# A last third of the tokens moved behind the attention: 72 interleaved items become 48 and three 512-token units, in a new written order

## The chip, the core and the metric

The kernel runs on one core of a Trainium2 chip. The metric is the device time of one execution in microseconds (us). Three runs of the kernel before gave 606.1, 606.41 and 606.9 us, median 606.41. Profiles are of one execution each, taken by the hardware profiler.

## The reference

An mLSTM attention (2 batches, 8 heads, 768 steps, head size 40) feeds two feed-forward layers, all in float32:

```python
for t in range(S):                       # attention, for each batch and head
    m_new = maximum(f[t] + m, i[t])
    C = exp(f[t] + m - m_new) * C + exp(i[t] - m_new) * outer(v[t], k[t])
    n = exp(f[t] + m - m_new) * n + exp(i[t] - m_new) * k[t]
    y[t] = sigmoid(o[t]) * (C @ q[t]) / maximum(abs(n @ q[t]), 1)
x = y as (1536, 320)
for e in range(4):                       # 320 -> 1024 -> 320, weighted by token
    out += p[:, e:e+1] * (maximum(x @ w1[e], 0) @ w2[e])
result = ((out @ w_a) * (out @ w_b)) @ w_out     # 320 -> 1536 -> 320
```

## The kernel before

**Tiles and chunks.** The 1536 tokens are 12 tiles of 128: tile n = 2j + b is chunk j (0 to 5) of batch b. The attention works chunk by chunk, since a chunk needs the state of the one before. The expert layer has 8 blocks of 512 hidden features, the last layer 6 blocks of 256. Every product is made of float32 values split into a rounded part (names in h: `xh`, `wh`, `hh`) and a rest (names in l), with three products for one.

**Two forms of the expert layer.** In the first stage blocks 0 to 2 are worked as *items* (class `Item`): one block, one group of 128 features, 256 tokens. An item has a first half (`a`, 8 matmuls of 256 columns, then `hh` on ScalarE and `hl` on VectorE) and a second half (`b`, 2 x 3 matmuls of 320 columns into `psy`). `Stream` lets the second halves run two items behind the first. The `psa` tiles of first halves have two PSUM banks, so the first half of item k needs the bank that `hl` of item k-2 has read. Twelve items cover 256 tokens, 72 all of them. In the second stage, from block 3 on, the work goes in *units* of one block and 512 tokens (`quad_a`, `quad_b`), in which two matmuls of 64 rows stand side by side.

**The order.** The attention steps lie between the items by a list `ev` of (time, step, arguments), line 711 on. A time k + 0.0 to k + 0.5 puts a step between the first half of item k and the second half of item k-2, a later one behind that second half. Each engine works what it gets strictly in this order, and so do the DMA queues of SP, ScalarE and GpSimd. For chunks 3 to 5 the list is made by a loop: chunk j is spread over twelve items that begin at 12 (j-1).

**Steps of one tile from chunk 2 on.** `load_qk` (DMA, three buffers), `split_qk` (ScalarE, line 356, rounds q and k into `qs`), four `low_qk` (VectorE or GpSimd, line 362, subtract the rounded values), `scores` (TensorE, `pt_c`), `spread_L` (line 425: a DMA that repeats a decay row over all partitions into `Rr`), `w_exp` (ScalarE, line 509, reads `Rr`), `w_mask` (GpSimd, line 513), `s1b` (VectorE, line 535: weights times scores), `s2a` (TensorE, `pt_y`, and `pt_i` with the state `cbd`), `s2b` and `s2x` (VectorE: y, x), `s2c` (copy), `s3a` (TensorE, transposes `pt_x`), `x_hi` (ScalarE) and `x_lo` (VectorE), which give `xh` and `xl` of that tile. `state`, `state_in`, `state_old`, `state_add` make the next state. `shift_x` (a DMA of GpSimd) makes `xq`, a shifted part of `xh`, for the units.

**Weights.** A block comes in 8 pieces: DMA, rounded copy (`wh`), rest (`wl`). The pieces of blocks 0 to 2 stand in `ev` (`go`), those of block 3 in the last 16 items, those of later blocks are paced by the units (`Paced`).

**Ends.** At the start chunk 0 runs alone: gates, a scan on VectorE (line 398), masks, scores, x, and the first item. At the end the last unit's four output tiles are added (line 847) and stored, one DMA each on SP's queue (line 851).

Of the kernel before, what the change touches and what calls it, by code (L numbers as in the profile page):

```python
# [50 lines left out]
def mlstm_moe_kernel(ctx, tc, gates, qk, qc, kvo, dp, w1b, w2b, ident_d, bdmask_d, rsel_d, exp_d, out):  # L51
# [262 lines left out]
    with ExitStack() as c1:  # L314
# [385 lines left out]
        def x_hi(n):  # L700
            split_hi(td[n]["pv"], n // 4, (n % 4) * P)

        def x_lo(n):
# [17 lines left out]
            (-34.8, gate1, 0), (-34.7, gate_d, 0, V), (-34.5, gate2, 0), (-34.4, hi_L, 0, V), (-34.3, low_L, 0),
            (-34.2, build_R, 0, V, 0, 4), (-34.15, gate_c, 0), (-34.1, hi_cm, 0, V), (-34.05, low_cm, 0), (-34, build_R, 0, A_, 4, 8),
            (-33.9, build_R, 1, V, 0, 4), (-33.8, build_R, 1, A_, 4, 8),
            (-33, weights_of, 0, 0), (-32.9, w_exp, 0, 0), (-32.7, weights_of, 0, 1), (-32.6, w_exp, 0, 1),
            (-32.5, scores2, 1), (-32.4, weights_of, 1, 0), (-32.3, w_exp, 1, 0), (-32.1, weights_of, 1, 1), (-32, w_exp, 1, 1),
# [289 lines left out]
```

## Time and profile before

| what | us |
|---|---|
| median of 3 runs | 606.41 |
| profiled execution | 606.0 |
| its span, first to last instruction | 604.3 |
| chunk 0 alone, to the first item | 0 to 17.2 |
| items with the attention between, to the first unit | 17.2 to 198.25 |
| units | 198.25 to about 596 |
| last output tiles and stores | to 604.3 |

The columns of the rows below: an engine's busy time is the time in which it works on an instruction; an idle time is put down to the engine or DMA whose signal ended it. PE is TensorE, DVE VectorE, ACT ScalarE, POOL GpSimd, SP the queue that issues most DMAs. TensorE's granted clock is 1.00 of full speed in every stretch shown.

### The profile page before, as it was taken

Reading aid. Unit: us, or ns where it says so; the run is one execution under the profiler, and the core shown is the slowest. Engines: PE = TensorE matmul, PEld = TensorE weight load, DVE = VectorE, ACT = ScalarE, POOL = GpSimd, SP = SyncE. Lnnn points to the kernel's source line nnn. Section 1 sums busy time; section 2 is a strip of 40 time slices with the busy share of each in tenths; the row PEclk is TensorE's granted clock in tenths of the full one; section 3 lists DMA queues with packets and bytes.
Section 4 is the critical chain, followed back from the end, with each engine's and each line's share of the span. In section 5 each row is a group of like instructions: output and inputs, shape, how many; then the busy total and the mean of one; then the engine's idle time right before and its main releaser. Section 6 shows DMA issues by size and latency. Waiting matters only on the chain.

```text
span 604.3 us, 14381 instructions
## 1 busy us (share of the span) xinstructions
PE 593.8 (98%) x5813; PEld 561.1 (93%) x5814; DVE 403.5 (67%) x821; ACT 273.3 (45%) x630; POOL 193.0 (32%) x248
## 2 busy tenths in 40 slices
PE   8999999999999999999999999999999999999997
PEld 5888999999999899999999999988898989888886
DVE  6898777776553333322799899898776787864444
ACT  7857475757433224333443434454553434341211
POOL 3966436272401011333234334332222121310000
PEclk9999999999999999999999999999999999999999
DMA  8967554746011223222222222222121121200012
GB/s 244 306 188 177 149 157 122 184 111 199 23 34 49 61 53 81 74 64 77 59 74 75 60 74 72 61 52 61 47 57 38 38 57 29 67 1 2 2 44 88
DMA packets 29344, 51.51 MB, mean 85 GB/s; under 512 B 3509, under 2 KB 18141, under 8 KB 29277
## 3 DMA queue, kind: packets, MB, share of 16 engines
q1 hardware_dynamic: 16045, 27.01, 16.3%
q10 hardware_dynamic: 12320, 21.22, 13.2%
q0 software_dynamic: 912, 2.36, 1.4%
q8 instruction: 46, 0.75, 0.5%
q14 instruction: 21, 0.17, 0.1%
HBM read 47.79 MB, written 2.00 MB: 82 GB/s over the span
## 4 chain that ended last, share of the span: by engine, by line
PE 93%; DVE 3%; POOL 1%; ACT 1%; DMA 1%; issue 0%; DVEq 0%
PE psy L261 27%; PE psa L236 27%; PE psb L236 11%; PE psa L216 10%; PE psy L295 3%; PE psy L297 3%; PE psy L296 3%; PE pt_y L545 3%; PE pt_i L551 1%; PE pt_c L531 1%; POOL wl L101 1%; PE pt_u L606 1%; DVE qs_t L362 1%; DMA gt<-in_gates 1%; PE pt_x L153 1%
## 5 line engine op out<-in xcount | busy, mean ns | idle before, releaser
L261 PE MATMUL psy<-wh,hl 64*128 64x320 f32 x752 | 139.9, 306 | 0.0
L261 PE MATMUL psy<-wh,hh 64*128 64x320 f32 x752 | 139.8, 306 | 0.0
L261 PE MATMUL psy<-wl,hh 64*128 64x320 f32 x752 | 139.8, 306 | 0.0
L236 PE MATMUL psa<-xh,wh 64*128 64x512 f32 x576 | 137.2, 389 | 0.0
L236 PE MATMUL psa<-xh,wl 64*128 64x512 f32 x414 | 99.0, 387 | 0.0
L261 PEld LDWEIGHTS psy<-wl,hh 64*128 64x128 f32 x752 | 94.0, 184 | 0.8
L261 PEld LDWEIGHTS psy<-wh,hh 64*128 64x128 f32 x752 | 94.0, 184 | 0.7
L261 PEld LDWEIGHTS psy<-wh,hl 64*128 64x128 f32 x752 | 94.1, 184 | 0.0
L236 PEld LDWEIGHTS psa<-xh,wh 64*128 64x128 f32 x576 | 84.5, 184 | 5.7 <-issue 0.9
L236 PE MATMUL psa<-xl,wh 64*128 64x512 f32 x384 | 87.2, 387 | 0.0
L864 DVE SCALAR_TENSOR_TENSOR hl<-psa,hh 128x512 fp32r<-128x512 f32 x60 | 38.6, 685 | 54.6 <-ACT hh L863 54.4
L133 POOL TENSOR_TENSOR wl<-tp,lf 128x272 fp32r<-128x272 f32 x48 | 38.8, 808 | 112.6 <-DVE tp L132 110.9
L236 PE MATMUL psb<-xh,wh 64*128 64x512 f32 x216 | 69.5, 388 | 0.0
L236 PEld LDWEIGHTS psa<-xh,wl 64*128 64x128 f32 x414 | 62.7, 184 | 3.6
L236 PEld LDWEIGHTS psa<-xl,wh 64*128 64x128 f32 x384 | 57.2, 184 | 3.5
L101 POOL TENSOR_TENSOR wl<-raw,wh 128x352 fp32r<-128x352 f32 (+1 forms) x30 | 28.1, 940 | 94.5 <-ACT wh L77 68.1
L236 PE MATMUL psb<-xh,wl 64*128 64x512 f32 x180 | 58.2, 387 | 0.0
L130 POOL TENSOR_TENSOR lf<-lf,sq 128x272 f32<-128x272 f32 x48 | 38.1, 793 | 62.9 <-ACT wh L129 48.9
L284 DVE SCALAR_TENSOR_TENSOR hl<-psa,hh 128x256 fp32r<-128x256 f32 x72 | 30.2, 421 | 41.2 <-ACT hh L283 40.7
L283 ACT ACTIVATE hh<-psa 128x256 fp32r<-128x256 f32 x72 | 27.5, 382 | 65.4 <-PE psa L216 64.7
L863 ACT ACTIVATE hh<-psa 128x512 fp32r<-128x512 f32 x60 | 32.5, 594 | 43.9 <-PE psy L261 26.7
L216 PE MATMUL psa<-xh,wh 128*128 128x256 f32 x216 | 51.3, 292 | 0.4 <-ACT xh L141 0.4
(144 smaller groups left out, 1416.5 us busy)
## 6 DMA issues: line engine op xcount, KB each, us to landing
raw<-in_w2b ACTq DMA_DIRECT2D x48, 272.0 KB, 2.8
qk_t<-in_qk SPq DMA_DIRECT2D x16, 480.0 KB, 6.8
raw<-in_w1b ACTq DMA_DIRECT2D x32, 176.0 KB, 2.3
acc<-in_w1b SPq DMA_DIRECT2D x22, 176.0 KB, 4.5
kvo_t<-in_kvo SPq DMA_DIRECT2D x10, 364.5 KB, 5.3
og_t<-in_kvo SPq DMA_DIRECT2D x6, 320.0 KB, 4.8
out<-acc SPq DMA_DIRECT2D x12, 160.0 KB, 2.6
qc_t<-in_qc SPq DMA_DIRECT2D x10, 180.0 KB, 3.6
```

The source lines that it names most:

```text
L101: lo_eng.tensor_tensor(wl[:, ps], raw[:, k * st // parts:(k + 1) * st // parts], wh[:, ps].bitcast(F32), op=ALU.subtract)
L130: nc.gpsimd.tensor_tensor(lf, lf, sq, op=ALU.mult)
L133: nc.gpsimd.tensor_tensor(wl[:, cs], tf, lf, op=ALU.add)
L216: nc.tensor.matmul(ps, l, r, start=(i == 0), stop=(i == len(prs) - 1))
L236: return nc.tensor.matmul(ps[g], w[rows, o:o + P], x, start=start, stop=stop)
L261: ms = [nc.tensor.matmul(ps[t], l[rows, t * P:(t + 1) * P], w[rows, off:off + DM], start=start, stop=stop) for t, rows in zip(two, (UP, DN))]
L283: nc.scalar.activation(self.hh, ps, AF.Relu)
L284: nc.vector.scalar_tensor_tensor(self.hl, ps, 0.0, self.hh.bitcast(F32), op0=ALU.max, op1=ALU.subtract)
L295: nc.tensor.matmul(ps, lh, wh[:, off:off + DM], start=(fi == 0), stop=False)
L296: nc.tensor.matmul(ps, lh, wl[:, off:off + DM], start=False, stop=False)
L863: nc.scalar.activation(hh, ps[f], AF.Relu)
L864: nc.vector.scalar_tensor_tensor(hl, ps[f], 0.0, hh.bitcast(F32), op0=ALU.max, op1=ALU.subtract)
```

## The change

Blocks 0 to 2 of tiles 8 to 11 (the last 512 tokens) are no longer worked as items. They become three units behind the 48 items that are left, ahead of block 3. The attention of all six chunks now stands between 48 items, in one list that is written out to its end. The pieces of block 3 are loaded during those three units, by a pace of their own. The first chunk's gates come in two DMAs, rows 0 to 63 on SP's queue and the rest on ScalarE's, there behind a load of keys and queries. The first matmuls of an item take the rest of the weights earlier; x of tile 1 is multiplied in two halves and rounded in three copies. The last output tile is made, added and stored in two halves of 160 columns, the second on ScalarE's queue. Block 1 now adds to the sum (VectorE) where block 0 has set it (tiles 8 to 11).

```diff
 NI = 12
+NCH1 = 4
...
         prs = [
-            (k(wh, 0), x(xh, 0)), (k(wh, 1), x(xh, 1)), (k(wl, 0), x(xh, 0)), (k(wl, 1), x(xh, 1)),
+            (k(wh, 0), x(xh, 0)), (k(wl, 0), x(xh, 0)), (k(wh, 1), x(xh, 1)), (k(wl, 1), x(xh, 1)),
             (k(wh, 0), x(xl, 0)), (k(wh, 1), x(xl, 1)), (k(wh, 2), x(xh, 2)), (k(wl, 2), x(xh, 2)),
         ]
...
         e = blk // 2
-        if blk <= 1:
+        if blk == 0 or blk == 1 and n < 4 * NCH1 // 2:
             nc.scalar.activation(acc[n], ps, AF.Copy, scale=pg[:, n, 0:1])
         else:
             nc.vector.scalar_tensor_tensor(acc[n], ps, pg[:, n, e:e + 1], acc[n], op0=ALU.mult, op1=ALU.add)
...
             if j == 0:
                 nc.vector.memset(gt[:, 1, 0:1], NEG)
-                eng.dma_start(gt[:, :, 1:], gates[:, :, 0:P])
+                for e, r in zip(eng, (slice(0, 64), slice(64, G))):
+                    e.dma_start(gt[r, :, 1:], gates[r, :, 0:P])
             else:
                 eng.dma_start(gt, gates[:, :, j * P - 1:(j + 1) * P])
...
-                nc.vector.tensor_tensor(xv, xu, r, op=ALU.mult)
+                for p in range(parts):
+                    hs = slice(p * H // parts, (p + 1) * H // parts)
+                    nc.vector.tensor_tensor(xv[:, hs], xu[:, hs], r[:, hs], op=ALU.mult)
...
-        def x_hi(n):
-            split_hi(td[n]["pv"], n // 4, (n % 4) * P)
+        def x_hi(n, apart=False):
+            if apart:
+                for k in range(3):
+                    nc.scalar.copy(xh[n // 4][:, k, (n % 4) * P:(n % 4 + 1) * P], td[n]["pv"][:, k])
+            else:
+                split_hi(td[n]["pv"], n // 4, (n % 4) * P)
...
-            (-40, load_gates, 0, A_), (-39.9, load_rsel, nc.sync), (-39.8, load_qk, 0, 0, A_), (-39.7, load_qk, 0, 1, nc.sync),
...
+            (-40, load_qk, 0, 1, A_), (-39.9, load_gates, 0, (nc.sync, A_)), (-39.8, ones, ), (-39.7, table, AF.Exp), (-39.6, load_qk, 1, 1, A_),
...
-            w3.extend(block1(3, wp1))
+            w3.extend(piece1(3, s, wp1, nc.vector if LOENG[3][s] == "v" else nc.gpsimd, True, nc.scalar) for s in range(NP1))
...
-        ev += [(56, block3)] + [(2 * NI * (c + 1) - NI + 1.95, shift_x, c) for c in range(3)]
-        for f in range(NP1):
-            ev += [(56.9 + 1.5 * f + d, lambda f=f: go(w3[f:f + 1])) for d in (0, 1.3, 1.7)]
...
-        for k in range(NI * NCH):
+        for k in range(NI * NCH1):
...
         until(1e9)
+        block3()
...
-    paced = Paced(pieces, PACE)
+    paced, early = Paced(pieces, PACE), Paced(w3, ((0, 2.0),))
...
-    units = [(blk, c) for blk in range(3, NB1 + NB2) for c in range(3)]
+    units = [(blk, 2) for blk in range(3)] + [(blk, c) for blk in range(3, NB1 + NB2) for c in range(3)]
     last = None
     for u, (blk, c) in enumerate(units):
         at = (14, 29) if blk >= NB1 else (7, 14, 22, 29)
-        ready = u - 2 - 3 * (NB1 - 4)
+        ready = u - 2 - 3 * (NB1 - 3)
+
+        turn = early if u < 3 else paced
 
         def hook(j):
             if j in at:
-                paced.step()
+                turn.step()
             if j == 15 and 0 <= ready < 3:
...
+        n, parts = 4 * c + t, 1 + t // 3
+        for p in range(parts):
+            cs = slice(p * DM // parts, (p + 1) * DM // parts)
+            ps = pa.tile([P, 512], F32, tag="a", name="psy")[:, 0:DM // parts]
+            for f in range(2):
+                hh, hl = (x[:, t * P:(t + 1) * P] for x in h[f])
+                wo, lo = (w[:, f * WF2 + 768:f * WF2 + 768 + DM][:, cs] for w in (wh, wl))
+                nc.tensor.matmul(ps, hh, wo, start=f == 0, stop=False)
+                nc.tensor.matmul(ps, hh, lo, start=False, stop=False)
+                nc.tensor.matmul(ps, hl, wo, start=False, stop=f == 1)
+            nc.vector.tensor_tensor(acc[n][:, cs], ps, acc[n][:, cs], op=ALU.add)
+            r0 = n % 2 * S + n // 2 * P
+            (nc.scalar if p else nc.sync).dma_start(out[r0:r0 + P, cs], acc[n][:, cs])
```

Three places in the order of instructions. TensorE, where the items end and the units begin (`psa` of 256 columns belongs to items, of 512 to units; `xh_75` and `xh_77` are the first and the last third of the tokens; `wh_156`, `wh_157` are block 0, `wh_361`, `wh_354` block 2, `wh_2444` block 3). Before:

```order
L295 MATMUL psy<-wh_361,hh 128x320
L296 MATMUL psy<-wl_362,hh 128x320
L297 MATMUL psy<-wh_361,hl 128x320
L295 MATMUL psy<-wh_361,hh 128x320
L296 MATMUL psy<-wl_362,hh 128x320
L297 MATMUL psy<-wh_361,hl 128x320
L236 MATMUL psa<-xh_75,wh_2444 128x512 x4
L236 MATMUL psa<-xh_75,wl_2445 128x512 x4
L236 MATMUL psa<-xl_78,wh_2444 128x512 x4
```

Now:

```order
L293 MATMUL psy<-wh_354,hh 128x320
L294 MATMUL psy<-wl_355,hh 128x320
L295 MATMUL psy<-wh_354,hl 128x320
L293 MATMUL psy<-wh_354,hh 128x320
L294 MATMUL psy<-wl_355,hh 128x320
L295 MATMUL psy<-wh_354,hl 128x320
L234 MATMUL psa<-xh_77,wh_157 128x512 x4
L234 MATMUL psa<-xh_77,wl_158 128x512 x4
L234 MATMUL psa<-xl_80,wh_157 128x512 x4
```

The unit that follows the last item is now block 0 on the last third of the tokens. In the new order the transposes of tile 11 stand one and a half items ahead of that unit; in the old one 13 items lay between the transposes of tile 11 and the first unit, which read the first third.

VectorE in chunk 2, from `hl` of item 11 on (`cbd_t` is `state_in` of tile 3, `qs_t` are `low_qk`, `w_t` is `s1b`). Before, the first `qs_t` row is tile 4, head group 0, the next two are group 1:

```order
L284 SCALAR_TENSOR_TENSOR hl_832<-psa_833,hh_831 128x256
L614 TENSOR_TENSOR cbd_t_848<-pt_u_844,bdmask_106 120x369
L362 TENSOR_TENSOR qs_t_826<-qk_t_692,qs_t_826 40x512
L362 TENSOR_TENSOR qs_t_852<-qk_t_711,qs_t_852 40x512 x2
L284 SCALAR_TENSOR_TENSOR hl_875<-psa_876,hh_874 128x256
L398 SCALAR_TENSOR_TENSOR fa_898<-gt_783,fa_588 112x128
L284 SCALAR_TENSOR_TENSOR hl_904<-psa_905,hh_903 128x256
L306 SCALAR_TENSOR_TENSOR acc_84<-psy_815,pg_69,acc_84 128x320
```

Now (`qs_t_867` is tile 4, head group 1; `qs_t_920` tile 5, head group 0; group 0 of tile 4 stands ahead of this piece):

```order
L282 SCALAR_TENSOR_TENSOR hl_834<-psa_835,hh_833 128x256
L615 TENSOR_TENSOR cbd_t_859<-pt_u_846,bdmask_106 120x369
L360 TENSOR_TENSOR qs_t_867<-qk_t_679,qs_t_867 40x512
L282 SCALAR_TENSOR_TENSOR hl_878<-psa_879,hh_877 128x256
L397 SCALAR_TENSOR_TENSOR fa_892<-gt_760,fa_590 112x128
L534 TENSOR_TENSOR w_t_871<-pt_c_902,w_t_871 128x512
L360 TENSOR_TENSOR qs_t_867<-qk_t_679,qs_t_867 40x512
L282 SCALAR_TENSOR_TENSOR hl_923<-psa_924,hh_922 128x256
L360 TENSOR_TENSOR qs_t_920<-qk_t_850,qs_t_920 40x512 x2
L304 SCALAR_TENSOR_TENSOR acc_84<-psy_820,pg_69,acc_84 128x320
L304 SCALAR_TENSOR_TENSOR acc_84<-psy_821,pg_69,acc_84 128x320
```

The subtractions of tile 5 and the first `s1b` have moved up by about one item, ahead of two additions to the sum.

GpSimd and ScalarE where the decay row of tile 8 is fetched and read (`Rr0` is `Rr` of batch 0; on GpSimd the masks `w_t` are those of tile 7, on ScalarE `w_t_1747` before and `w_t_1559` now are `w_exp` of tile 8). GpSimd before:

```order
L513 AFFINE_SELECT w_t_1417<-w_t_1417 128x512
L513 AFFINE_SELECT w_t_1512<-w_t_1512 128x512
L620 TENSOR_TENSOR cbd_t_1116<-cbd_t_1116,dec_114 120x369
L594 TENSOR_TENSOR kw_t_1550<-kvo_t_1240,ET_1278 128x360
L425 DMA Rr0_110<-dL_t_1434 128x1024
L628 TENSOR_TENSOR cbd_t_1555<-cbd_t_1555,cbd_t_1116 120x369
L620 TENSOR_TENSOR cbd_t_1195<-cbd_t_1195,dec_114 120x369
```

GpSimd now, the DMA directly behind the masks of tile 7:

```order
L595 TENSOR_TENSOR kw_t_1401<-kvo_t_1001,ET_1203 128x360
L512 AFFINE_SELECT w_t_1430<-w_t_1430 128x512
L512 AFFINE_SELECT w_t_1408<-w_t_1408 128x512
L424 DMA Rr0_110<-dL_t_1370 128x1024
L629 TENSOR_TENSOR cbd_t_1446<-cbd_t_1446,cbd_t_1140 120x369
L621 TENSOR_TENSOR cbd_t_1145<-cbd_t_1145,dec_114 120x369
L629 TENSOR_TENSOR cbd_t_1526<-cbd_t_1526,cbd_t_1145 120x369
```

ScalarE before, ahead of the first `w_exp` that reads the row:

```order
L283 ACTIVATE hh_1675<-psa_1677 128x256
L141 CAST xh1_76<-pt_x_1701 128x3x128
L473 COPY ET_1708<-pt_e_1662 128x96
L475 COPY dec_114<-pt_e_1662 120x17
L283 ACTIVATE hh_1711<-psa_1713 128x256
L356 CAST qs_t_1724<-qk_t_1629 120x1024
L283 ACTIVATE hh_1734<-psa_1736 128x256
L509 ACTIVATE w_t_1747<-Rr0_110,ET_1708 128x128 x4
L283 ACTIVATE hh_1770<-psa_1772 128x256
```

ScalarE now, behind the last `w_exp` of tile 7:

```order
L281 ACTIVATE hh_1467<-psa_1469 128x256
L142 CAST xh1_76<-pt_x_1463 128x3x128
L354 CAST qs_t_1493<-qk_t_1483 120x1024
L370 ACT_TABLE_LOAD
L370 ACTIVATE og_t_1343<-og_t_1343 128x640
L658 ACTIVATE warm_127<-rmask_107 1x1
L658 ACT_TABLE_LOAD
L658 ACTIVATE warm_127<-rmask_107 1x1
L281 ACTIVATE hh_1534<-psa_1536 128x256
L472 COPY ET_1555<-pt_e_1530 128x96
L474 COPY dec_114<-pt_e_1530 120x17
L508 ACTIVATE w_t_1559<-Rr0_110,ET_1555 128x128 x4
```

From the last `w_exp` of tile 7 to the first of tile 8 ScalarE had seven `hh` of items before, and has two now; the DMA has moved from behind the weights of a state to behind both masks.

## Rows read from the trace of the kernel before

**Rows 1.** The page, busy time by engine.

```profile
PE 593.8 (98%) x5813; PEld 561.1 (93%) x5814; DVE 403.5 (67%) x821; ACT 273.3 (45%) x630; POOL 193.0 (32%) x248
```

**Rows 2.** Busy time by stretch: start:end, length, each engine, clock, DMA share, GB/s.

```profile
17.20:53.00 35.80, 33.63 (x258) 31.72 (x259) 31.65 (x68) 25.45 (x59) 27.98 (x45) 1.00 0.81 230
53.00:198.25 145.25, 144.30 (x1146) 143.71 (x1144) 93.37 (x198) 81.71 (x201) 56.79 (x62) 1.00 0.44 115
```

**Rows 3.** What TensorE waited for, 17 to 200 us: total, times, longest.

```profile
PE pt_i L551 <- DVE cbd_t L614: 1.2, 1, 1.2
PE pt_c L531 <- DVE qs_t L362: 0.9, 1, 0.9
PE pt_x L153 <- DVE x_t L585: 0.6, 1, 0.6
PE psa L216 <- ACT xh L141: 0.4, 1, 0.4
```

**Rows 4.** Chain of waits, four stretches: start us, us, what.

```profile
100.52 0.40 PE pt_c L531 x4
...
105.92 1.75 PE pt_y L545 x16
107.67 0.70 PE pt_i L551 x6
...
192.73 0.96 PE psa L216 x8
...
194.57 0.96 PE psa L216 x8
...
249.12 6.83 PE psa L236 x60
255.95 7.04 PE psy L261 x96
```

**Rows 5.** Groups by line with one shape: busy us, mean ns, idle before.

```profile
L284 DVE SCALAR_TENSOR_TENSOR hl<-psa,hh 128x256 fp32r<-128x256 f32 x72 | 30.2, 421 | 41.2 <-ACT hh L283 40.7
...
L535 DVE TENSOR_TENSOR w_t<-pt_c,w_t 128x512 f32<-128x512 f32 x24 | 16.2, 683 | 2.2 <-POOL w_t L513 1.2 <-ACT w_t L505 1.0
...
L614 DVE TENSOR_TENSOR cbd_t<-pt_u,bdmask 120x369 f32<-120x369 f32 x10 | 5.4, 536 | 4.8 <-PE pt_u L606 4.8
```

**Rows 6.** Line 362, subtraction of the rounded keys and queries: min/median/max ns.

```profile
L362 DVE TENSOR_TENSOR qs_t<-qk_t,qs_t x18: 673/690/1819, 52.5 to 152.5; 40x512 fp32r<-40x512 f32 x18
L362 POOL TENSOR_TENSOR qs_t<-qk_t,qs_t x14: 1265/1458/1807, 52.5 to 156.3; 40x512 fp32r<-40x512 f32 x14
```

**Rows 7.** Timeline of VectorE, three of these in a row.

```profile
52.48 4.25 DVE L362 TENSOR_TENSOR qs_t<-qk_t,qs_t 40x512 fp32r<-40x512 f32 x3
```

**Rows 8.** DMAs of the decay row: all, at 103 and 134 us: KB, landing.

```profile
Rr<-dL_t POOLq DMA_DIRECT2D x3, 512.0 KB, 9.2
Rr<-dL_t ACTq DMA_DIRECT2D x3, 512.0 KB, 4.3
...
Rr<-dL_t POOLq DMA_DIRECT2D x1, 512.0 KB, 10.4
...
Rr<-dL_t POOLq DMA_DIRECT2D x1, 512.0 KB, 7.1
```

**Rows 9.** Timeline of GpSimd and ScalarE, chunk 3, batch 0.

```profile
68.02 0.63 POOL L513 TENSOR_SCALAR_AFFINE_SELECT w_t<-w_t 128x512 f32<-128x512 f32 x1
68.60 0.61 POOL L425 DMA_DIRECT2D Rr<-dL_t  x1
...
86.10 0.38 ACT L283 ACTIVATE hh<-psa 128x256 fp32r<-128x256 f32 x1 [0.52 <-PE psa L216]
86.38 1.27 ACT L509 ACTIVATE w_t<-Rr,ET 128x128 f32<-128x128 f32 x4
```

**Rows 10.** Timeline of VectorE, first wait and last instruction.

```profile
4.21 0.43 DVE L398 TENSOR_TENSOR_SCAN fa<-gt 112x128 f32<-112x128 f32 x1 [2.98 <-DMA gt<-in_gates]
...
600.10 0.49 DVE L847 TENSOR_TENSOR acc<-psy,acc 128x320 f32<-128x320 f32 x1 [0.39 <-PE psy L911]
```

More of the change, by code (lines that the diff above doesn't have):

```diff
@@ L721, in mlstm_moe_kernel @@
[L721 to L725, printed above, removed]
@@ new lines, in mlstm_moe_kernel @@
+            (11.443, state_in, 3), (11.667, split_qk, 4, 1), (11.733, state_add, 3), (11.8, low_qk, 4, 1, 0, V), (11.867, w_exp, 4, 0),
+            (11.933, w_mask, 4, 0), (12.157, load_qk, 5, 1), (12.214, gate1, 3), (12.271, w_exp, 4, 1), (12.329, scores, 4, 0),
+            (12.386, w_mask, 4, 1), (12.443, load_kvo, 5), (12.7, s1b, 4, 0), (12.8, low_qk, 4, 1, 1, V), (12.9, split_qk, 5, 0),
+            (13.18, shift_x, 0), (13.26, low_qk, 5, 0, 1, V), (13.34, low_qk, 5, 0, 0, V), (13.42, w_exp, 5, 0), (13.8, s2a, 4, 0),
@@ new lines, in mlstm_moe_kernel @@
+            (14.144, scores, 4, 1), (14.189, s1b, 4, 1), (14.233, split_qk, 5, 1), (14.278, w_mask, 5, 0), (14.322, gate_d, 3, nc.gpsimd),
+            (14.367, w_exp, 5, 1), (14.411, gate2, 3), (14.456, scores, 5, 0), (14.733, load_kvo, 6), (14.867, gate4, 3), (15.129, weigh_k, 5),
+            (15.157, s2a, 4, 1), (15.186, s2b, 4), (15.214, low_qk, 5, 1, 0, nc.gpsimd), (15.243, gate_c, 3), (15.271, send_L, 3, nc.sync),
+            (15.3, gate5, 3), (15.329, load_o, 3, nc.sync), (15.357, low_qk, 5, 1, 1, nc.gpsimd), (15.386, load_qk, 6, 0), (15.414, weigh_k, 4),
@@ new lines, in mlstm_moe_kernel @@
+            (15.443, s1b, 5, 0), (15.471, s2x, 4), (15.68, state_old, 4), (15.76, w_mask, 5, 1), (15.84, scores, 5, 1), (15.92, s1b, 5, 1),
+            (16.3, table, AF.Sigmoid), (17.3, split_qk, 6, 0), (17.627, s2a, 5, 0), (17.653, state, 4), (17.68, s2a, 5, 1), (17.707, s2c, 4, P_),
+            (17.733, s3a, 4), (17.76, state, 5), (17.787, load_qk, 6, 1), (17.813, x_hi, 4), (17.84, split_qk, 6, 1), (17.867, state_in, 4),
+            (17.893, spread_L, 6, nc.gpsimd), (17.92, x_lo, 4), (17.947, state_in, 5), (17.973, low_qk, 6, 0, 0, V), (18.64, gate_tail, 3),
@@ new lines, in mlstm_moe_kernel @@
+            (24.38, s2x, 6), (24.42, weigh_k, 7), (24.46, gate_c, 4), (24.68, state_old, 6), (24.76, weigh_k, 6), (24.84, scores, 7, 0),
+            (24.92, w_exp, 7, 1), (25.15, state, 6), (25.2, w_exp, 7, 0), (25.25, s2c, 6, nc.scalar), (25.3, load_kvo, 8), (25.35, scores, 7, 1),
+            (25.4, w_mask, 7, 0), (25.45, state_in, 6), (25.657, w_mask, 7, 1), (25.714, s1b, 7, 0), (25.771, spread_L, 8, nc.gpsimd),
+            (25.829, gate4, 4), (25.886, gate5, 4), (25.943, s3a, 6), (26.18, state_add, 6), (26.26, x_hi, 6), (26.34, s1b, 7, 1),
@@ new lines, in mlstm_moe_kernel @@
+            (28.68, load_gates, 5), (28.72, x_hi, 7), (28.76, x_lo, 7), (28.8, gate1, 5), (28.84, w_exp, 8, 1), (28.88, load_qk, 9, 0),
+            (28.92, low_qk, 8, 0, 0, nc.gpsimd), (28.96, low_qk, 8, 0, 1, nc.gpsimd), (29.3, split_qk, 8, 1), (29.8, w_mask, 8, 0),
+            (30.2, low_qk, 8, 1, 1, V), (30.3, low_qk, 8, 1, 0, nc.gpsimd), (30.4, w_mask, 8, 1), (30.64, split_qk, 9, 0), (30.68, scores, 8, 0),
+            (30.72, s1b, 8, 0), (30.76, weigh_k, 8), (30.8, low_qk, 9, 0, 1, nc.gpsimd), (30.84, load_o, 5, nc.sync), (30.88, load_qk, 9, 1),
@@ new lines, in mlstm_moe_kernel @@
+            (30.92, w_exp, 9, 1), (30.96, low_qk, 9, 0, 0, V), (31.657, scores, 8, 1), (31.714, s1b, 8, 1), (31.771, gate_d, 5, nc.gpsimd),
+            (31.829, split_qk, 9, 1), (31.886, gate2, 5), (31.943, send_L, 5, nc.sync), (32.2, gate_c, 5), (32.3, gate4, 5), (32.4, gate5, 5),
+            (32.65, s2a, 8, 0), (32.7, s2a, 8, 1), (32.75, scores, 9, 0), (32.8, s2b, 8), (32.85, low_qk, 9, 1, 1, nc.gpsimd),
+            (32.9, low_qk, 9, 1, 0, V), (32.95, s2x, 8), (33.8, load_kvo, 10), (34.131, w_mask, 9, 1), (34.162, scores, 9, 1), (34.192, s1b, 9, 1),
```

162 lines of the change are left out of this document (75 added, 87 removed).

## The prediction

> **What bounds the kernel now.** I read the busy times first: TensorE works 593.8 us of a span of 604.3 [rows 1], so a change gains only by taking matmul time away, by taking away waits of TensorE, or at the two ends. Then the busy times by stretch: from 53 us to the first unit TensorE works 144.30 of 145.25 us, while VectorE is busy 64% and ScalarE 56% [rows 2]; from 17.2 to 53 us it works 33.63 of 35.8. Third, what TensorE waited for: four waits that sum to 3.1 us [rows 3]; the 0.95 us that it is idle behind 53 us is the wait for `qs`, 0.9, so no other lies there, at a granted clock of 1.00. So the prices of items and units decide, and then whether the attention, now between 48 items, still comes in time. The profiled execution took 606.0 us; the median of the runs, 606.41, is 0.4 above it.
>
> **Items to units.** An item costs 1.84 us: two first halves (0.96 each) stand 1.84 apart in the chain, with a second half of 0.88 between [rows 4]. A unit costs 6.83 + 7.04 = 13.87 us [rows 4]. Out go 24 x 1.84 = 44.16 us, in come 3 x 13.87 = 41.61: -2.55 us. This is the firm term. Block 3's pieces, loaded among the items before, go beside the three units, where only the units' own `hh` and `hl` stand. Block 1's additions for tiles 8 to 11 go to VectorE in the same place, four instructions, and cost nothing there.
>
> **The cover of the attention.** From item 12 to the first unit TensorE now has 145.25 - 44.16 - 0.9 = about 100.2 us of work. VectorE had 93.4 us in that stretch and loses the `hl` of 24 items, 24 x 0.42 = 10.1 [rows 2, 5]: 83.3 left, 83% of the stretch instead of 64%. ScalarE has 81.7 - 9.2 (24 `hh` of 0.38 [rows 9]) = 72.5, 72%. No engine becomes full in the mean, but VectorE had 88% from 17.2 to 53 us [rows 2], and that is where all waits of TensorE stood. So I expect waits, and go through the places one by one.
>
> **Chunk 1.** The wait for the state of tile 0 (1.2 us) shrinks, since the order puts that state ahead of the scores of tile 3, but the queue of VectorE ahead of it is unchanged: 0 to 1.2, I take 0.6. The wait for x of tile 3 (0.6) goes, for its instruction has moved up; 0.3 stay at the first item.
>
> **Chunk 2.** The piece of VectorE's order in the part on the change shows the race. TensorE needs, from the end of the first half of item 11 to the scores of tile 5, three first halves, three second halves, two scores of 0.40, a quarter of `pt_y` (1.75) [rows 4] and two small pieces of about 0.5 together: 2.9 + 2.6 + 0.8 + 0.4 + 0.5 = 7.2 us. VectorE can begin 0.8 later (`hh` 0.38, `hl` 0.42), so it has 6.4 us for: state 0.54, two `hl` 0.84, a scan 0.43, `s1b` 0.68 [rows 5, 10], 2.5 in all, and four `low_qk`. Of these the trace shows 0.69 in the median and up to 1.82 [rows 6], and three in a row that took 4.25, 1.42 each [rows 7]. That gives 5.3 to 9.8 us, a wait of 0 to 3.5. At 1.2 each it is 7.3, a wait of 0.9; I take 1.0, where it was 0.9. GpSimd works beside VectorE here, as it did in the row of 1.42, and that is why I don't take the median.
>
> The Trainium skill ("SBUF — State Buffer", section "Who interferes with whom") says that a VectorE instruction with two SBUF inputs contends with a GpSimd instruction that reads SBUF, and that the later one is fully blocked. By that rule each of the 18 `low_qk` of VectorE could take its 0.69 and one of GpSimd's 1.46 us, 26 us more in all, and the stretch would be VectorE's: (83.3 + 26) / 0.88 = 124 us, a kernel of about 626. The trace agrees only in part: three in a row at 1.42 us and a longest of 1.82 show such a thing, but a median of 0.69 shows that most met nothing of the kind.
>
> **The decay row of tile 8.** Before, the DMA left at 68.60 for a reader of chunk 3 at 86.38 [rows 9], 17.8 us later. Now it leaves behind both masks of tile 7, and the reader is two `hh` behind the `w_exp` that these masks wait for. From the end of item 25's first half the chain is: `hh` 0.38, `w_exp` 1.27, two masks of 0.63, issue 0.61 [rows 9], landing, `w_exp` of tile 8 1.27, `hh` 0.38, `hl` 0.42: 5.6 us and the landing. TensorE reaches item 30, which needs the bank of that `hl`, after four first halves, five second halves, one scores 0.40, half of `pt_y` 0.87, half of `pt_i` 0.35 [rows 4] and five small pieces, four of them of three matmuls like that half, some 1.5 together: 11.3 us. Landings of this DMA: 4.3 on ScalarE's queue; 9.2, 10.4 and 7.1 on GpSimd's [rows 8]. The wait is then 0 to 4.7 us; with 7.1, the nearest to it since it is of this queue and from the least loaded of the three stretches, it is 1.4, and I take that. It is a new wait: ScalarE stands at `w_exp`, and the `hh` of item 28 stands behind it.
>
> **The rest of the stretch.** The other spreads have leads of over 10 us of matmuls. In chunks 3 to 5 a step's inputs now often end within one item of their reader (tile 11: y, x and its copy behind `pt_i`, about as long as the matmuls between, and then the shift of x that the first unit reads). I put 0.6 there, 0 to 2. Sum of waits: 0.3 + 0.6 + 1.0 + 1.4 + 0.6 = 3.9 in place of 3.1: +0.8.
>
> **Start.** The first scan waits 2.98 us for the gates and begins at 4.21 [rows 10]. They now come in halves; the second half stands behind a load of keys on ScalarE's queue, so the scan could start earlier by 0.8 (half the bytes) or later by 1.5 (a landing of 4.3 behind an issue, as the row of that queue [rows 8] bounds it). I take 0 there, and -0.1 for the finer steps of tile 1, x in two halves and a rounding in three copies.
>
> **Tail.** The last addition (0.49) begins at 600.10 [rows 10], and the span ends at 604.3, so the last store takes 3.7 us from there. Six last matmuls of 0.147 become twelve of 160 columns, each between 0.07 (by columns) and 0.12 (an item's matmul of 256, 0.96 / 8): 0 to +0.6, I take +0.4. The half addition lies between 0.25 and 0.49, I take -0.2. Half the bytes on a queue of its own: 0 to -1, I take -0.4. Together -0.2, between -0.7 and +0.5.
>
> **Sum.** 606.0 - 2.55 + 0.8 - 0.1 - 0.2 = 603.95, and 0.4 more for the median: 604.4 us.
>
> **The rivals.** *The waits go.* The new order may be dense and still timely: landings of 4.3, `low_qk` of 0.69. TensorE would keep about 1 us of waits, -2.1 instead of +0.8: 604.4 - 2.9 = 601.5. For it: one wait of TensorE from 53 us on, with VectorE 64% busy; against it: the new share is 83%. *The gain is given back.* The decay row lands in 9.2 us as in the median of its queue, +2.1 on the forecast: 606.5, no change. For it: three landings of three above 7; against it: those were in stretches full of other loads. *VectorE becomes the bound, slower.* Place: chunks 2 to 5. If `low_qk` take 1.42 us on VectorE throughout, as three of them did, its work is 83.3 + 18 x 0.73 = 96.4 us; at the 88% that it reached before, the stretch lasts 109.6 us, where the forecast has 100.2 + 3.0. That is +6.4: 610.8. It decides from a mean of about 1.26 on: then the work is 93.6, the stretch 106.4 and the kernel at 607.6. Against it: the median of 0.69. That units don't cost 13.87 at the new place is unlikely: the pieces of a unit are the same matmuls there.
>
> **How the numbers follow.** This measurement can tell about 0.2% from no change, 1.2 us: faster is below 605.2, slower above 607.6. Forecast 0.42 (own range 603.2 to 605.5), waits gone 0.20, given back 0.21, slower 0.17, of which a part is the decay row at 10.4 with chunk 2 at its upper bound (604.4 + 3.3 + 2.5 = 610). The ends of the range, 600.8 and 607.8, take in the first three cases with the start and tail at their good bounds, and leave out most of the fourth. Faster: nearly the whole forecast and the waits gone, 0.60; no change 0.22; slower 0.18.
>
> **What would show it.** The first unit should begin near 17.2 + 181.05 - 44.16 + 0.8 = about 155 us, and units cost 13.87 us there too. In the list of TensorE's waits: one for the scores of tile 5, and one for an `hl` of item 28 with ScalarE idle before the first `w_exp` of tile 8 until its decay row lands; nothing over 1 us elsewhere. VectorE at 80 to 85% from item 12 on, `low_qk` with a median below 0.8. The scan near 4.2 us; the last store within 4 us of the last addition. If the first unit begins after 158 us, the pressed order is the reason and the rival on VectorE or on the decay row is told by those two rows; if it begins before 153, the waits have gone. If it begins at 155 and the time is still not below 605.2, the ends are wrong.

## The result and the profile after

The changed kernel took 611.67 us (median of 4 runs, 611.02 to 614.09), the kernel before 606.56 in the same comparison: a ratio of 1.0092 with a 95% interval of 1.0064 to 1.012. It is slower by about 5 us. The forecast was 604.4, with a range of 600.8 to 607.8. The profiled execution of after took 614.09 (span 612.3, the longest of the four; the others had 609.2 to 610.1). The spans of the two profiled executions, 612.3 and 604.3, are 8.0 us apart, and that is the sum to be explained here. Since this execution of after is the slowest of its four, 2 to 3 us of the sum are not in the other three; which part of it they lack no profile shows.

The page of after, busy time by engine and the clock that TensorE was granted in 40 slices:

```profile
PE 601.3 (98%) x5951; PEld 567.3 (93%) x5952; DVE 402.3 (66%) x813; ACT 268.2 (44%) x614; POOL 196.3 (32%) x256
PEclk8699899999999999999999999999999999999999
```

TensorE is as full as before [rows 1], 98%, but it is busy for 7.5 us more. The second line says why a busy share must not be read alone: in the first two slices and around 65 us the clock is below full, and a matmul that runs at half the clock counts as busy for longer: the 32 `pt_y` of the chains below take 6.75 us instead of 3.54.

The chain of waits of after, the first 30 us (start us, us, what):

```profile
1.25 4.92 DMA gt<-in_gates
...
10.13 1.19 PE pt_a L499 x2
...
13.34 1.15 PE pt_a L499 x2
14.49 6.75 PE pt_y L544 x32
...
26.00 3.75 PE psa L214 x24
```

The same of before:

```profile
0.81 3.30 DMA gt<-in_gates
...
8.19 0.70 PE pt_a L500 x2
...
9.98 0.66 PE pt_a L500 x2
10.64 3.54 PE pt_y L545 x32
...
17.19 2.25 PE psa L216 x16
```

TensorE's idle time (in brackets) ahead of the first decay weights of before, from its timeline, and its busy time by stretch (columns as in the table of after below):

```profile
8.19 0.70 PE L500 MATMUL pt_a<-Rr,LT 112*128 112x512 f32 x2 [1.16 <-DVE LT L443]
```

```profile
8.00:12.00 4.00, 3.81 (x34) 3.27 (x35) 2.94 (x6) 3.36 (x8) 2.78 (x6) 1.00 1.08 327
12.00:16.00 4.00, 4.00 (x41) 3.46 (x41) 3.53 (x12) 3.51 (x8) 1.60 (x5) 1.00 1.06 326
```

The half of the gates that stands behind the keys on ScalarE's queue is issued at 1.25 and lands 4.92 us later; the scan begins at 6.29 instead of 4.21 [rows 10]. The first decay weights are 1.94 us later (10.13 against 8.19). From there to the first item the same matmuls take 15.87 us instead of 9.00: `pt_y` takes 6.75 for 3.54, almost twice. The first item is 8.8 us late.

Busy time by stretch of after (start:end, length, PE, PEld, DVE, ACT and POOL with their counts, granted clock, DMA share, GB/s):

```profile
4.00:8.00 4.00, 3.84 (x23) 2.29 (x21) 1.11 (x4) 0.90 (x1) 0.41 (x1) 1.00 1.07 277
8.00:12.00 4.00, 1.86 (x8) 1.32 (x10) 3.84 (x8) 3.44 (x8) 1.78 (x4) 0.72 1.09 306
12.00:26.00 14.00, 14.00 (x74) 12.21 (x71) 6.81 (x19) 6.42 (x16) 6.08 (x13) 0.50 0.80 233
26.00:53.00 27.00, 27.00 (x215) 26.05 (x215) 24.52 (x57) 21.47 (x52) 20.41 (x34) 0.98 0.59 164
...
62.00:63.00 1.00, 0.36 (x3) 0.09 (x1) 0.87 (x2) 0.00 (x0) 0.78 (x2) 1.00 1.03 259
66.00:67.00 1.00, 0.00 (x0) 0.00 (x0) 0.99 (x3) 1.00 (x5) 0.21 (x1) 1.00 0.94 234
68.00:71.00 3.00, 3.00 (x14) 3.00 (x14) 2.96 (x5) 1.09 (x4) 2.85 (x4) 0.50 0.02 6
```

TensorE is idle for 2.1 of the four us from 8 on, and then works without a pause at 0.50, the lower of its two levels (1.2 GHz), for the whole stretch from 12 to 26 us, where before has 1.00. The other engines idle through it: VectorE is at 6.81 of 14. The same happens for 3 us at 68, behind idle times at 62 to 67.

What TensorE waited for in after, up to 170 us (total, times, longest):

```profile
PE pt_a L499 <- DVE LT L442: 2.3, 1, 2.3
PE pt_c L530 <- DVE qs_t L360: 2.1, 2, 1.7
...
PE pt_y L544 <- issue: 0.9, 1, 0.9
```

Three of the four waits of [rows 3] are gone, and the one for `qs` has grown: it is 1.67 us at 67.44 and 0.42 at 141.33, where before had 0.9. With the 0.94 us ahead of `pt_y` at 63.30, chunk 2 has 2.6 us of waits. The 8.0 us then split so: first item +8.8; from the first item to the first unit 138.2 us (26.0 to 164.17), where before has 198.25 - 17.19 - 44.16 = 136.9, +1.3; items to units -2.55; the rest of the kernel, 612.3 - 164.17 - 41.61 = 406.5 against 604.3 - 198.25 = 406.05, +0.5. The sum is +8.0.

The mean granted clock of an execution is either about 1.00 or about 0.985 here, and the kernel before takes some 6 us longer in the second kind. All four runs of after are of the second kind (0.982 to 0.986). Of the runs of the kernel before in the three comparisons below 8 of 78 are (611.7 to 612.2 us), all others of it lie between 605 and 607.8. None of the 8 was profiled; that their clock fell at the start, as in the profiled ones of other kernels, is likely and not shown.

### The profile page after: what moved, and what is told of

Its sections match the earlier page's. It is cut to its first block, busy times and chain, and to the rows that moved or that the text cites. A ratio compares the mean times of both kernels' runs of the same rounds, so it can differ in the third digit from the quotient of the medians.

```text
span 612.3 us, 14645 instructions
## 1 busy us (share of the span) xinstructions
PE 601.3 (98%) x5951; PEld 567.3 (93%) x5952; DVE 402.3 (66%) x813; ACT 268.2 (44%) x614; POOL 196.3 (32%) x256
## 4 chain that ended last, share of the span: by engine, by line
PE 95%; DMA 2%; DVE 1%; ACT 1%; issue 0%; ACTq 0%; POOL 0%; SPq 0%; DVEq 0%
PE psy L259 30%; PE psa L234 30%; PE psb L234 11%; PE psa L214 7%; PE pt_y L544 4%; PE psy L293 2%; PE psy L295 2%; PE psy L294 2%; DMA kvo_t<-in_kvo 1%; PE pt_i L550 1%; PE pt_c L530 1%; PE pt_u L607 1%; PE pt_c L522 1%; DMA gt<-in_gates 1%; DVE qs_t L360 1%; PE pt_x L154 1%
## 5 line engine op out<-in xcount | busy, mean ns | idle before, releaser
L259 PE MATMUL psy<-wl,hh 64*128 64x320 f32 x848 | 158.5, 306 | 0.0
L259 PE MATMUL psy<-wh,hl 64*128 64x320 f32 x848 | 158.4, 306 | 0.0
L259 PE MATMUL psy<-wh,hh 64*128 64x320 f32 x848 | 158.2, 306 | 0.0
L234 PE MATMUL psa<-xh,wh 64*128 64x512 f32 x648 | 150.3, 389 | 0.0
L234 PE MATMUL psa<-xh,wl 64*128 64x512 f32 x468 | 109.6, 387 | 0.0
L259 PEld LDWEIGHTS psy<-wh,hh 64*128 64x128 f32 x848 | 106.9, 184 | 0.7
L259 PEld LDWEIGHTS psy<-wl,hh 64*128 64x128 f32 x848 | 106.7, 184 | 0.7
L259 PEld LDWEIGHTS psy<-wh,hl 64*128 64x128 f32 x848 | 106.7, 184 | 0.0
L886 DVE TENSOR_TENSOR g<-psa,bs 128x512 f32<-128x512 f32 x36 | 24.8, 688 | 38.9 <-ACT bs L885 38.6
L130 ACT CAST wh<-tp 128x272 fp32r<-128x272 f32 x48 | 20.2, 420 | 67.5 <-DVE tp L127 67.5
L885 ACT COPY bs<-psb 128x512 f32<-128x512 f32 x36 | 21.0, 583 | 60.9 <-PE psb L234 60.9
```

The source lines that it names most:

```text
L130: nc.scalar.copy(wh[:, cs], tf)
L234: return nc.tensor.matmul(ps[g], w[rows, o:o + P], x, start=start, stop=stop)
L259: ms = [nc.tensor.matmul(ps[t], l[rows, t * P:(t + 1) * P], w[rows, off:off + DM], start=start, stop=stop) for t, rows in zip(two, (UP, DN))]
L885: nc.scalar.copy(bs, ps[2 * f])
L886: nc.vector.tensor_tensor(g, ps[2 * f + 1], bs, op=ALU.mult)
```

## The experiments

**Whose is the late start?** The new first chunk was put into the kernel before, and the old one into the kernel after. The first edit exchanges all entries of `ev` ahead of the first item, with the gates in two loads:

```diff
-            (-40, load_gates, 0, A_), (-39.9, load_rsel, nc.sync), (-39.8, load_qk, 0, 0, A_), (-39.7, load_qk, 0, 1, nc.sync),
+            (-40, load_qk, 0, 1, A_), (-39.9, load_gates, 0, (nc.sync, A_)), (-39.8, ones, ), (-39.7, table, AF.Exp), (-39.6, load_qk, 1, 1, A_),
...
```

> The kernel before, with the new first chunk's list (gates in two loads, the second behind a load of keys) but x of tile 1 multiplied and rounded in one piece. Theory C: the clock falls to 0.50 at about 10 us as in the kernel after, first item at 25 to 26.5 us, time 611 to 615, less what the other engines gain in those 8.8 us (a part of the 3.1 us of waits). Rival G (the late gates cost their own 2 us and no more): first item at 19 to 20 us, time 607 to 609.

Measured: 613.85 us (4 runs, 612.92 to 614.93) against 606.46, ratio 1.0115 (1.0061 to 1.017). Its first item began at 26.0. Busy time by stretch of this kernel:

```profile
8.00:12.00 4.00, 1.87 (x6) 1.15 (x8) 3.84 (x8) 3.69 (x8) 1.67 (x3) 0.66 1.08 295
12.00:26.00 14.00, 14.00 (x75) 12.22 (x73) 6.44 (x18) 6.37 (x14) 6.19 (x13) 0.50 0.83 232
```

Theory C has it: without any of the units and without the new order, the first chunk alone costs more than the whole loss, with the clock at 0.50. The other way round, with the old list in the kernel after:

> The kernel after, with the first chunk's list (loads, gates in one load, masks, all up to the first item) put back to that of before; from the first item on it is the kernel after. Theory C (TensorE's clock: the late gates leave TensorE idle for 2.3 us at 7.8 us, its granted clock goes to 0.50 until 26 us, and that costs most of the 8.8 us by which the first item is late): first item at 17.2 to 17.6 us, granted clock 1.00 up to 53 us, time 603 to 606. Rival O (the new order of the items is what costs, by the loads of chunk 2 and 3 that land late at 58 to 67 us): time 608 or more, and the stall of TensorE between 58 and 68 us is still there.

Measured: 605.13 us (10 runs), ratio 0.999 (0.9955 to 1.0024). This is theory C in the median, but the profiled execution (610.13) fell, with an idle time of 1.09 us where before has 1.16, and two others did:

```profile
8.85 0.87 PE L499 MATMUL pt_a<-Rr,LT 112*128 112x512 f32 x2 [1.09 <-DVE LT L442]
```

```profile
8.00:12.00 4.00, 3.15 (x19) 2.43 (x20) 2.61 (x6) 2.48 (x8) 2.45 (x5) 0.65 1.07 334
12.00:26.00 14.00, 13.86 (x66) 12.18 (x67) 6.47 (x17) 7.09 (x14) 6.47 (x15) 0.50 0.81 254
```

The seven executions that kept the clock have a median of 604.97; the 21 of before that kept it, in the same comparison, 606.13. So where the clock holds, the units with the new order gain about 1.2 us. The first item that was expected at 17.2 to 17.6 us is not shown, since the execution that was profiled fell (its first item began at 24.5); of rival O it has a wait of 1.4 us for `qs`. With nearly the same idle time the kernel before mostly keeps the clock, so it stands at the edge of the fall itself.

**Is it the clock, or are the gates just late?** Ten matmuls of zeros were put where TensorE waits for the gates, which still come late:

```diff
-            (-36.3, mask_of, 1, 0, ps_a, "a"), (-36.2, scores2, 0), (-36.1, mask_of, 1, 1),
+            (-36.3, mask_of, 1, 0, ps_a, "a"), (-36.2, scores2, 0), (-36.15, warm_up, 10, pw), (-36.1, mask_of, 1, 1),
...
```

> The kernel after, with ten more matmuls of zeros (512 columns, 0.2 us each at full clock) between the scores of tile 0 and the last mask, where TensorE waits for the gates. The gates come as late as before. Theory C: granted clock 1.00 from 4 to 53 us, first item at 19 to 20.5 us (the 2.1 us of the late gates are left), time 604 to 607. Rival G (the chain of the gates through VectorE and ScalarE is late by itself and TensorE's speed doesn't matter there): first item still behind 24 us, time within 1 us of 611.7.

Measured: 606.22 us (10 runs, 604.78 to 607.79), mean clock 0.996 to 1.00 in all of them, ratio 0.9987 (0.9958 to 1.0016). The scan began at 6.23, as late as in after. Busy time by stretch:

```profile
8.00:12.00 4.00, 3.41 (x24) 1.87 (x24) 3.84 (x8) 3.75 (x8) 1.72 (x4) 1.00 1.08 297
12.00:26.00 14.00, 13.86 (x109) 11.84 (x106) 11.86 (x32) 11.93 (x28) 11.00 (x22) 1.00 1.07 285
```

The first item began at 19.3. Work that computes nothing makes the kernel 5.4 us faster; rival G is out. It also splits the 8.8 us: 2.1 are left when the clock holds, as much as the scan is late (2.0), and 6.7 are the clock. The rest of this kernel: 137.3 us from the first item to the first unit (156.6), +0.4 on the kernel before.

**What makes the gates late?** The gates first, ahead of the keys:

```diff
-            (-40, load_qk, 0, 1, A_), (-39.9, load_gates, 0, (nc.sync, A_)), (-39.8, ones, ),
+            (-40, load_gates, 0, (nc.sync, A_)), (-39.9, load_qk, 0, 1, A_), (-39.8, ones, ),
...
```

> The kernel after, with both halves of the gates issued first, ahead of the keys on ScalarE's queue. Theory C: the scan begins at 4 to 4.8 us instead of 6.29, TensorE's idle time before the decay weights is 1 to 1.6 us, the clock stays at 1.00, first item at 17.5 to 18.5, time 603 to 606. Rival Q (not the place in the queue but the load in halves or the other loads beside it delays the gates): scan at 5.5 us or later, clock 0.50, time above 609.

Measured: 611.29 us (10 runs), ratio 1.0066 (1.0028 to 1.0104). The scan began at 3.48, earlier than in before, and the clock fell in all ten all the same. Both my theories were wrong on this one: the gates' place does set the gates, but there is a second late load. The timeline of ScalarE and that of TensorE:

```profile
6.63 2.00 ACT L699 ACTIVATE Rr<-rsel 48x1024 fp32r<-48x1024 f32 x2 [2.72 <-DMA rsel<-in_rsel_d]
```

```profile
8.68 0.49 PE L499 MATMUL pt_a<-Rr,LT 112*128 112x512 f32 x1 [0.65 <-ACT Rr L699]
9.98 0.80 PE L499 MATMUL pt_a<-Rr,LT 112*128 112x512 f32 x1 [0.81 <-ACT Rr L481]
```

A table of 7 KB, `rsel`, which the new list issues behind larger loads on SP's queue, lands at 6.6, ScalarE builds its rows behind it, and TensorE idles twice. The two idle times, 1.5 us together, lie within the 1 to 1.6 for which theory C expected the clock to hold, so the sum of idle time alone did not tell what the clock does. So the table was put first as well (`(-41, load_rsel, nc.sync)`):

> The kernel after, with the small table (rsel, 7 KB) issued first on SP's queue and both halves of the gates ahead of the keys; with the gates alone ahead, the scan began at 3.48 us but ScalarE still waited for rsel until 6.63, TensorE was idle for 1.5 us in two pieces, and the clock fell. Theory C: rsel now lands before 4 us, ScalarE builds its rows in time, TensorE's idle time before the first decay weights is below 1 us, the clock stays at 1.00, first item at 17 to 18 us, time 603 to 606. Rival S (something else of the new list lets the clock fall, such as the later masks): idle above 1.2 us or the clock at 0.50 all the same, time 609 or more.

Measured: 607.61 us (604.61 to 611.02 in 10 runs), ratio 1.0037 (1.0012 to 1.0063), between the two theories. In the profiled execution TensorE idled 0.6 us, the clock was full up to 61 us and the first item began at 18.1:

```profile
8.66 0.69 PE L499 MATMUL pt_a<-Rr,LT 112*128 112x512 f32 x2 [0.58 <-DVE LT L442]
```

But in four executions of ten the mean clock was 0.985 to 0.988, and one more took 610.15 us at 0.999. The six that kept it have a median of 606.3, where before has 605.5. The new first chunk is no gain even without its late loads; why the clock fell in these four no profile shows.

**Does filling the gap make it safe?** Five matmuls of zeros in the gap of the old first chunk (the last mask moves behind them, by its time of -34.88), once with the new order and once in the kernel before:

```diff
-            (-35, mask_of, 0, 0, ps_b, "b"), (-34.95, mask_of, 0, 1, ps_b, "b"), (-34.93, mask_of, 1, 0, ps_a, "a"), (-34.92, mask_of, 1, 1),
-            (-34.9, scores2, 0),
+            (-35, mask_of, 0, 0, ps_b, "b"), (-34.95, mask_of, 0, 1, ps_b, "b"), (-34.93, mask_of, 1, 0, ps_a, "a"), (-34.88, mask_of, 1, 1),
+            (-34.9, scores2, 0), (-34.89, warm_up, 5, pw),
```

> The old first chunk's list with the new order behind it, as in the run with the old start, and five more matmuls of zeros between the scores of tile 0 and the last mask, where TensorE was idle for 1.1 us and the clock fell in 3 executions of 10. Theory C: the clock stays at 1.00 in all executions, time 604 to 605.5 in each, median about 604.8 (where the held executions of the old start lay). Rival: some still fall, to 610 or more.

> The kernel before with five more matmuls of zeros between the scores of tile 0 and the last mask. The kernel before idles there for 1.16 us, and 4 of its 25 executions in the last comparison took 612 us at a mean granted clock of 0.985. Theory C: no execution falls, median 606.1 to 606.6 (the held ones of before lie at 606.1), span as before. Rival: the falls have another cause (and come as often), or the extra matmuls delay the start by up to 1 us.

Measured: with the new order 604.91 us (602.83 to 607.68), ratio 0.9988 (0.9973 to 1.0004), clock 0.994 to 1.00 in ten of ten; in the kernel before 607.02 (606.03 to 607.63), 1.0023 (1.0011 to 1.0034), and no fall in nine. With the new order the falls go (three of ten without the matmuls). For the kernel before, nine executions can't show it, as in this comparison only one of 30 fell without them; and there the matmuls aren't free: the 29 that kept the clock without them have a median of 605.5, 1.5 us less. Its first item begins only 0.1 us later (17.33); TensorE has a second wait for `low_qk`, 1.11 us at 63.36, which the kernel before doesn't have, and why is open. The spread of the kernel with the new order is wider than the 604 to 605.5 that I expected.

**The wait in chunk 2.** With the early start the wait at 53 to 64 us was still there (TensorE busy 8.60 of 11 us with the new order and the gap filled), so it isn't the late start's. In after, the timelines of ScalarE, TensorE and VectorE, and the DMA issues from 53.5 to 54.5 us:

```profile
64.22 1.05 ACT L354 CAST qs_t<-qk_t 120x1024 fp32r<-120x1024 f32 x1 [2.79 <-DMA qk_t<-in_qk]
65.17 0.38 ACT L281 ACTIVATE hh<-psa 128x256 fp32r<-128x256 f32 x1
```

```profile
63.30 1.09 PE L544 MATMUL pt_y<-kvo_t,w_t 128*128 128x82 f32 x8 [0.94 <-issue]
...
67.44 0.78 PE L530 MATMUL pt_c<-qs_t 120*128 120x128 f32 x4 [1.67 <-DVE qs_t L360]
```

```profile
62.13 0.48 DVE L397 TENSOR_TENSOR_SCAN fa<-gt,fa 112x128 f32<-112x128 f32 x1 [1.42 <-DMA gt<-in_gates]
```

```profile
qk_t<-in_qk SPq DMA_DIRECT2D x1, 480.0 KB, 10.5
gt<-in_gates SPq DMA_DIRECT2D x1, 112.9 KB, 9.2
```

The list puts the rounding of tile 5's keys at time 12.9, ahead of item 13. Its load takes 10.5 us to land, with the DMA engines full, and the rounding stands in ScalarE's order ahead of the `hh` of an item whose matmuls have long ended. VectorE then waits for `hh`, with two `low_qk` behind it, and TensorE for these. The 0.94 us at 63.30 have another late load behind them: the scan of the next gates waits 1.42 us on VectorE, ahead of the `s1b` that `pt_y` needs. The edit moves the rounding, its two `low_qk` and its scores back, the rounding by one item, in the kernel with the ten extra matmuls (the entries that change, cut out of their lines):

```diff
-(12.9, split_qk, 5, 0)
-(13.26, low_qk, 5, 0, 1, V), (13.34, low_qk, 5, 0, 0, V)
-(14.456, scores, 5, 0)
+(13.9, split_qk, 5, 0)
+(13.95, low_qk, 5, 0, 1, V), (13.96, low_qk, 5, 0, 0, V)
+(15.0, scores, 5, 0)
```

> The kernel after with the ten extra matmuls (clock held, 606.2), and the rounding of the keys of tile 5, head group 0, on ScalarE moved by one item (its subtractions on VectorE and its scores behind it), so that the hh of items 13 doesn't stand behind a rounding that waits for a load. Theory W (ScalarE's order makes the wait of 1.8 us at 60 to 64 us, since hh stands behind a rounding whose keys land 10 us after their issue): this wait of TensorE falls below 0.8, time 604.8 to 605.7. Rival L (the loads themselves are too late, whatever stands behind them): the same 1.5 to 2 us turn up at the scores of tile 5, time 606 to 606.8.

Measured: 604.28 us (603.57 to 604.77 in ten runs), ratio 0.9967 (0.9945 to 0.9989), where 606.22 was the kernel without this edit, in another comparison. The stretch from 53 to 64 us, without the edit and then with it:

```profile
53.00:64.00 11.00, 9.21 (x73) 8.93 (x72) 8.06 (x16) 8.21 (x22) 7.29 (x10) 1.00 0.74 177
```

```profile
53.00:64.00 11.00, 10.60 (x86) 10.13 (x84) 9.28 (x16) 8.52 (x23) 7.64 (x11) 1.00 0.78 189
```

TensorE's idle time there goes from 1.8 to 0.4 us, its wait for `qs` from 1.78 to 0.18, and the two spans are 604.6 and 602.9. That is theory W, with a time 0.5 below its range. The 1.9 us between the medians are too many for the edit: against the executions of before that kept the clock, each in its own comparison (606.1 and 605.5), the kernel without the edit is 0.1 above and this one 1.2 below, and those 1.3 us agree with the idle time.

**Both causes taken away.** Old first chunk, five extra matmuls, the rounding one item later, and once more with the last tile in one piece (`parts = 1`):

> The new order with the old first chunk's list, five extra matmuls ahead of the last mask, and the rounding of tile 5's keys one item later. If the two causes add (late start with the clock, 1.5 to 2 us by the gates alone; ScalarE's queue behind the keys, 1.9 us): first item at 17.3 to 17.7, first unit at 153 to 153.8, no execution falls, time 602.2 to 603.3, 2.2 to 3.3 below the kernel before (605.5 to 606.1 where its clock holds). If they don't add (the wait at 53 to 64 us was a consequence of the late start): 604 to 605.

> The same with the last output tile in one piece (six matmuls of 320 columns, one addition, one store on SP's queue, as before). The traces so far have the end of the kernel after, from the last unit's first matmul on, 0.3 to 0.5 us longer than that of before; if the two halves are the reason, this run is 0.3 to 0.5 us below the one with them. Rival, as forecast: the halves gain 0.2, and this run is 0.2 above.

Measured: 603.17 us (12 runs, 601.92 to 605.13) against 606.18, ratio 0.9944 (0.9918 to 0.9969), and 603.07 with the tail in one piece, 0.9952 (0.9926 to 0.9977). The two causes add as expected, and this version beats both kernels: 3 us below before (2.8 below its executions that kept the clock), 8.5 below after. In its profile:

```profile
53.00:64.00 11.00, 11.00 (x90) 10.73 (x88) 10.03 (x17) 6.92 (x19) 9.09 (x12) 1.00 0.55 139
```

The first item begins at 17.6, the first unit at 153.7. The tail's two forms are 0.1 us apart, inside either spread: this question stays open. The profiled execution of the second one took 606.27, far above its median, and mostly not by its tail: its first item began at 19.97, 2.3 us later, though its mean granted clock is 1.00. The 16 scores of tile 0 take 2.08 us there, where before takes 1.16 for its own (5.87), so durations have to be read beside the clock:

```profile
6.72 2.08 PE L522 MATMUL pt_c<-qk_t 40*128 40x128 f32 x16 [0.46 <-DMA qk_t<-in_qk]
```

## Why the prediction was wrong, by its own steps

**Start: the step that failed.** It said "I take 0 there, and -0.1", between -0.8 and +1.5. Measured: +8.8, of which 2.1 are the gates (the kernel with ten extra matmuls against before) and 6.7 the clock. Two errors. The bound of the late gates was too narrow: the half behind the keys landed after 4.92 us, and I had let 4.3 be the worst. And I read the granted clock, 1.00, as a constant of this kernel, when it was a result of how little TensorE paused in the first chunk; no rival had it. The price was in no row of before; what could have raised the question is the idle time of 1.16 us just ahead of a stretch in which all work waits for TensorE. The Trainium skill has such a case ("TensorE: Matmul & The Clock Gate", section "Loop structure matters more than you think"): among its examples a loop with a long DMA wait between every matmul is the one in which TensorE "goes cold". The trace agrees in kind, with a single wait: 0.50 from 12 to 26 us behind an idle time of 2.3.

The forecast's own sign would have misled as well: a first unit after 158 us was to show the pressed order as the reason. It began at 164.17 in after, and at 156.6 in the kernel with ten extra matmuls, where the clock held in the same pressed order.

**Items to units: right.** Units follow one another at 13.86 us (187.32 to 201.18), those of the new place too, with pieces of 6.83 and 7.04 as before [rows 4]:

```profile
187.32 6.83 PE psa L234 x60
194.14 7.04 PE psy L259 x96
201.18 6.83 PE psa L234 x60
```

**Waits: less than forecast, and in other places.** Forecast +0.8 from the first item to the first unit, measured +1.3 in after and +0.4 in the kernel with the ten extra matmuls. But the +1.3 are not waits. From 26.0 to 53 us TensorE of after never idles, and behind it for 3.0 us, no more than the 3.1 of before:

```profile
53.00:164.17 111.17, 108.14 (x854) 106.77 (x853) 84.52 (x175) 70.00 (x171) 60.29 (x71) 0.98 0.58 157
```

What came is work at half the clock: from 67.44 on the scores, a second half and a first half take 3.9 us up to the next `pt_y`, and 2.5 for the same in the kernel with the ten extra matmuls. In that kernel, whose clock holds, TensorE idles 1.0 us in chunk 1 (13.04 of 14 us busy from 26 to 40, and full from 40 to 53), where I put 0.9 with the first item, and 1.8 in chunk 2, where I put 1.0 (its upper bound of 3.5 should read 3.4 by its own terms). The larger idle time of chunk 1, 0.63 us at 35.04, is put down to GpSimd's `wl`, not to the state of tile 0. That of chunk 2 is not the length of the subtractions, but ScalarE's order behind a load. The decay row of tile 8, where I put 1.4, cost nothing: issued at 103.46, it landed 6.3 us later, below the 7.1 that I took [rows 8], and its reader began at 111.08, 1.3 us behind that. The DMA issue and the reader:

```profile
Rr<-dL_t POOLq DMA_DIRECT2D x1, 512.0 KB, 6.3
```

```profile
111.08 0.41 ACT L508 ACTIVATE w_t<-Rr,ET 128x128 f32<-128x128 f32 x1
```

**VectorE as the bound: did not come.** The rival needed a mean of 1.26 us for `low_qk`. Line 360 in after (min/median/max ns):

```profile
L360 DVE TENSOR_TENSOR qs_t<-qk_t,qs_t x18: 673/940/1523, 54.5 to 148.8; 40x512 fp32r<-40x512 f32 x18
L360 POOL TENSOR_TENSOR qs_t<-qk_t,qs_t x14: 1260/1284/1781, 69.0 to 149.1; 40x512 fp32r<-40x512 f32 x14
```

The median rose from 0.69 [rows 6] to 0.94, but the rival is about the mean, and that hardly moved: 0.92 us in before and 0.97 in after (busy us, mean ns):

```profile
L362 DVE TENSOR_TENSOR qs_t<-qk_t,qs_t 40x512 fp32r<-40x512 f32 x18 | 16.5, 920 | 0.8 <-ACT qs_t L356 0.5
```

```profile
L360 DVE TENSOR_TENSOR qs_t<-qk_t,qs_t 40x512 fp32r<-40x512 f32 x18 | 17.5, 974 | 0.5 <-ACT qs_t L354 0.3
```

The sum of this rival added 18 x 0.73 to the 83.3 us as if the 18 had taken their median before; from the mean it is 18 x 0.50, about 92.3 us of work and a stretch of 105, not 109.6. TensorE was busy for 59.99 of the 60 us from 80 to 140. The time came out slower, on the side of this rival, for a reason that this rival doesn't contain.

**Tail: within its bounds.** Forecast -0.2; the profiled pair says +0.5 for all behind the first three units, the pair of runs on the tail says 0.1. The twelve short matmuls (0.11 us each) and the short addition (0.33) came about as forecast; the last store took 4.0 us behind the addition in after, where 3.7 of before were to become 3.3.

Put together, with the old first chunk, its gap filled, and chunk 2's order mended the change is worth 3.0 us. That the forecast of 2.0 is near it is in part luck: of its waits the decay row's 1.4 us did not come, and those of chunks 1 and 2 came from other places.

## What to carry to other kernels

Read the granted clock as a result of the kernel's own pauses: ahead of any edit that makes TensorE wait longer at the start, ask what runs behind that wait at half speed, and try matmuls that compute nothing in the wait: they were worth 5.4 us where the clock fell, and cost 1.5 us in the kernel before, which mostly kept it. In an order written by hand, an instruction that waits for a load takes everything behind it on its engine along: look for the in-order engine on which a late load stands ahead of the next item's work. When loads are pressed together, take their landing times from stretches as full as the new ones, small tables too.
